# Reordering the prologue of an FFT convolution followed by two feed-forward layers

## The chip, the cores and the metric

The kernel runs on one core of one Trainium2 chip. The metric is the device time of one execution in microseconds (us). The kernel before took 1052.2 us (median of 3 runs, 1052.01 to 1052.93).

Five engines work side by side, each through its own list of instructions in order, and wait for each other by semaphores: TensorE (PE, matrix products), VectorE (DVE), ScalarE (ACT), GpSimd (POOL) and SyncE (SP, which here only issues DMAs).

## The reference, cut to what matters

```python
def _attn_ref(x, filt_r, filt_i):            # x: 2 x 3008 x 256
    X = np.fft.rfft(x, axis=1)
    Y = X * (filt_r + 1j * filt_i)[None, :, :]
    return np.fft.irfft(Y, n=x.shape[1], axis=1)

x = _attn_ref(x, ...).reshape(6016, 256)
h = x @ moe_w_in                             # 256 -> 2048
g = np.where(h > 0, h, np.exp(np.minimum(h, 0)) - 1)
x = g @ moe_w_out                            # 2048 -> 256
h = x @ moe2_w_in
g = h * np.clip(h + 3, 0, 6) / 6
return g @ moe2_w_out
```

A Fourier transform along each of two sequences, a complex product with a filter, the transform back, and two feed-forward layers on the 6016 rows that come out.

## The kernel before

The transform of length 3008 is split as 47 times 64, so that it becomes small matrix products with a transpose between them. A sequence is treated in two halves of 128 columns (h is 0 or 1). For the first sequence, whose work the change moves, each half goes through these steps; the letters are those of the string `PROLOGUE`, and the digits behind a letter are h and the group g:

- **A** (`s1t`): products with the 47-point table, five columns at a time, copied from PSUM into the tile zt. Seven groups; those of half 0 stand ahead of the string.
- **T** (`tr`): four transposes into one PSUM bank, and a copy out of it. Six groups a half.
- **S** (`s2_mm`, then `mult`): the 64-point product on PE (line 204), then the complex product with the filter: three VectorE multiplications (lines 216, 216, 217) and an addition on GpSimd (line 219).
- **I** (`i2_mm`, `i2_evac`): the inverse 64-point product (line 224), a ScalarE copy (line 234) and a DMA to a buffer in DRAM (line 235).
- **V** (`v_load`): four DMAs that read the half back from DRAM (line 239), transposed on the way. All six groups I of the half must have landed.
- **O** or **o** (`i1_mm`, `i1_evac`): the inverse 47-point products (line 247), seven groups a half, copied out on ScalarE (O) or VectorE (o) into the blocks from which the first layer reads.

Between them stand: **F**, the sign of a filter group on GpSimd (line 149), without which its complex product can't start; **c** and **k**, steps of the generators `lead` and `conv`, which turn chunks of the first layer's weights (int64 words of a double) into two rounded floats; **w**, the DMA of a raw chunk; **M**, the split of a table into two rounded floats; **x**, **b**, **B**, the load, the split and the first product of the second sequence; **X**, the split of a block into two rounded floats (line 85 has VectorE's half); **G** and **H**, the first and second half of the first layer's product of a block with chunk 0.

A chunk's conversion is five VectorE operations (lines 299, 300, 304, 306, 308) and one on ScalarE (297), then one ScalarE rounding (314) and two VectorE operations (316, 318). Chunk 0 must be ready before G.

Behind the string come the 96 units of the main loop, each of six first-layer products (lines 88 to 90), an ELU on ScalarE and VectorE (lines 497, 498, 500), a split (lines 84, 85) and, three units later, twelve second-layer products. From there on the two kernels hold the same instructions in the same order.

The order on each engine is the order in which the program issues it; nothing reschedules it. PSUM has seven banks in turn, so an instruction may also wait until a bank is read out. SP issues DMAs in the program's order, and each of its DMAs waits until the eighth before it has landed.

Of the kernel before, what the change touches and what calls it, by code (L numbers as in the profile page):

```python
# [47 lines left out]
def fft_conv_moe_moe2(ctx, tc, xp, fq, sg, cs1, cs1t, cs2, ci2, ci1, ident, w1i, w1o, w2i, w2o, out):  # L48
    nc = tc.nc
# [11 lines left out]
    def name(s):  # L61
        uid[0] += 1
        return f"{s}_{uid[0]}"
# [7 lines left out]
    def bank():  # L71
        return ps.tile([P, 512], F32, tag="ps", name=name("ps"))
# [81 lines left out]
    def s1t(b, h, jg, eng):  # L154
        if jg == 0:
            zt[h] = p12.tile([P, NK2, 2, 2, NJ], F32, tag="zt", name=name("zt"))
        acc = bank()
        j0, n = jg * TG, min(TG, NJ - jg * TG)
        for j in range(j0, j0 + n):
            nc.tensor.matmul(  # L160
                acc[:, (j - j0) * KP : (j - j0 + 1) * KP], xin[b, h, j // 8][:KP, j % 8, :],
                mats["s1t"][:KP], start=True, stop=True,
            )
        evac(
            eng,
            zt[h].rearrange("p k c h j -> p (c h) k j")[:, :, :, j0 : j0 + n],
            acc[:, : n * KP].rearrange("p (j c k) -> p c k j", j=n, c=4),
        )

    def tr(b, h, g, eng):  # L170
        acc = bank()
        for k in range(4):
            nc.tensor.transpose(
                acc[:, k * P : (k + 1) * P],
                zt[h][:, 4 * g + k].rearrange("p c h j -> p (c h j)"), mats["id"],
            )
        zs[b, h, g] = t2([P, 512])
        evac(eng, zs[b, h, g], acc)
# [665 lines left out]
    def fetch1(f):  # L844
# [9 lines left out]


    PROLOGUE = """
        T00 T01 T02 S00 T03 F01 S01 T04 F01 S02 T05 F01 S03 I00 F01 S04 I01 F01 A10 A11 F01
        S05 I02 A12 A13 A14 I03 F01 A15 A16 I04 T10 c01 T11 c01 w00 I05 F01 x00 x01 V00 T12
        S10 T13 S11 T14 F01 S12 T15 S13 I10 F01 S14 I11 S15 I12 O00 I13 b00 c01 O01 I14 c01
        b01 o02 O03 I15 M00 c01 b02 V10 c01 X00 O04 w01 b03 c01 X01 k02 O05 O06 X02 k02 B00  # L860
        B01 B02 B03 G00 G01 k03 O10 o11 G02 X10 o12 X11 O13 X12 o14 k02 H00 H01 k02 O15 k01
        H02 O16
    """
    LOADS = [(0, None, q, None) for q in range(4)]
    for x in "F00 F01 F02 F03 X0 X1 X2 X3 F04 F05 F10 W0 M F11 F12 F13 F14 F15".split():
# [150 lines left out]
    with tc.manual_schedule():  # L1016
        for key, src in (("s1t", cs1t), ("id", ident), ("sg", sg), ("s2", cs2), ("i2", ci2), ("i1", ci1)):
            load_mat(key, src)
        three = const.tile([P, 1], F32, name="three")
        nc.vector.memset(three, 3.0)  # L1020
        engs = (nc.scalar, nc.vector)

        acc = bank()
        for n in WARM:
            zeros = (nc.const_aps.tensor(0.0, [P, k], F32) for k in (P, n))
            nc.tensor.matmul(acc[:, :n], *zeros, start=True, stop=True)
        for h, g, q, r in LOADS:
            if q is not None:
                x_load(0, h, q)
            elif g is not None:  # L1030
                f_load(0, h, g)
            elif r is not None:
                w_raw(0, r)
            else:
                load_mat("s1", cs1, nc.sync)
        for jg in range(JG):
            s1t(0, 0, jg, engs[jg % 2])
        lead = w_chain(0, WLEAD, lambda f: None)
        f_sign(0, 0, 0)
        f_sign(0, 0, 1)  # L1040
        nsign = 2
        for step in PROLOGUE.split():
            what, h, g = step[:-2], int(step[-2]), int(step[-1])
            if what == "T":
                tr(0, h, g, nc.scalar if g > 1 else engs[g])
            elif what == "S":
                s2_mm(0, h, g)
                mult(0, h, g)
            elif what == "A":
                s1t(0, h, g, engs[g % 2])  # L1050
            elif what == "I":
                i2_mm(0, h, g)
                i2_evac(0, h, g)
            elif what == "V":
                for q in range(4):
                    v_load(0, h, q)
            elif what == "O":
                i1_mm(0, h, g)
                i1_evac(0, h, g, nc.scalar)
            elif what == "o":  # L1060
                i1_mm(0, h, g)
                i1_evac(0, h, g, nc.vector)
            elif what == "k":
                steps(conv, g)
            elif what == "c":
                steps(lead, g)
            elif what == "X":
                x_split(0, g, h)
            elif what == "F":
                for _ in range(g):  # L1070
                    f_sign(0, *divmod(nsign, 6))
                    nsign += 1
            elif what == "x":
                x_load(1, h, g)
            elif what == "w":
                w_raw(0, WLEAD + g)
            elif what == "b":
                s1_split(h, g)
            elif what == "B":
                s1_mm(1, h, g, parts.pop(("x", h, g)))  # L1080
                s1_evac(1, h, g)
            elif what == "G":
                g1_half(units[g], 0)
            elif what == "H":
                g1(units[g])
                if g:
                    g_split(units[g - 1])
            elif what == "M":
                split_mat("s1")

        for n, u in enumerate(units):
            place[0] = n
            for fn in pre[n]:
                fn()
            if n >= NI:
                g1(u)
                g_split(units[n - 1])
            if n >= SKEW:
                g2(units[n - SKEW])
            for fn in post[n]:  # L1100
                fn()
        def rest(n):
            def run():
                if n == NU:
                    g_split(units[-1])
                g2(units[n - SKEW])
                for fn in post[n]:
                    fn()
            return run

        old = None
        n = place[0] = NU
        for l, p in ROUNDS:
            for q in range(GROUPS):
                old = group(l, p, q, old, [rest(NU + i) for i in range(3)], pre[n : n + 4])
                n += 4
        prod(old.l, old.p, old.q, 3, old.c, False)
        old.high((1, 1))
        old.gate((1, 0))
        old.add((0, 1), old.u2, old.c)  # L1120
        old.low((1, 1))
        old.high((1, 0))
        old.relu((0, 1))
        old.low((1, 0))
        old.gate((0, 1))
        old.high((0, 1))
        old.low((0, 1))
        for key in ((0, 0), (1, 1), (1, 0), (0, 1)):
            old.second(key)
            if key == (1, 0):  # L1130
                out_evac(old.l, old.p, 0)
        out_evac(old.l, old.p, 1, True)
# [82 lines left out]
```

## Time and profile before

| | |
|---|---|
| median of 3 runs | 1052.2 us |
| the profiled execution | 1053.41 us, of which span 1051.6 us |
| PE busy | 1039.5 us (99%) |
| VectorE busy | 880.3 us (84%) |
| ScalarE busy | 807.4 us (77%) |
| GpSimd busy | 195.4 us (19%) |
| TensorE clock granted | 1.00 of full speed throughout |

The string's work lies in the first 72 us of the span. A timeline row names the start, the duration and the instruction, and in brackets how long the engine had been idle before it and what ended that. Matrix products are pipelined: a row's duration holds about 0.16 us of pipeline, so that the distance from start to start is the price of a product.

### The profile page before, as it was taken

The page shows a single profiled execution, that of the slowest core. Times are in us where ns is not written, and L with a number is a line of the kernel's source. Part 1 is how long each engine was busy: PE and PEld are TensorE (multiplying, and loading weights), DVE is VectorE, ACT ScalarE, POOL GpSimd, SP SyncE. Part 2 cuts the span into 40 slices and gives each one's busy share as a digit, 9 for nine tenths or more (in the row PEclk, how much of TensorE's full clock was granted, in tenths as well). Part 3 has the DMA queues.
Part 4 walks back from the last instruction along what each step waited for, and adds up shares of the span by engine and source line. Part 5 has one row for each costly group of instructions (what it writes and reads, how often), then busy time and mean ns, then how long its engine had stood idle before and what let it go on. Part 6 is the DMA issues. An engine that isn't in the chain of part 4 may idle for free.

```text
span 1051.6 us, 14389 instructions
## 1 busy us (share of the span) xinstructions
PE 1039.5 (99%) x5022; PEld 913.4 (87%) x5022; DVE 880.3 (84%) x1416; ACT 807.4 (77%) x1453; POOL 195.4 (19%) x211
## 2 busy tenths in 40 slices
PE   9999999999999999999999999999999999999998
PEld 6688888888889989988888888888888888888998
DVE  4899999789986888789989888888888888787776
ACT  3488888997777888888987877777777777777766
POOL 3700001425545933200011100010010010000000
PEclk9999999999999999999999999999999999999999
DMA  9993100474655543510564631100100100100100
GB/s 285 307 273 128 46 1 1 154 222 150 203 168 176 202 140 121 178 41 1 187 234 122 216 123 41 41 21 21 41 21 21 41 18 17 41 1 1 41 2 35
DMA packets 58056, 107.31 MB, mean 102 GB/s; under 512 B 5024, under 2 KB 33696, under 8 KB 57984
## 3 DMA queue, kind: packets, MB, share of 16 engines
q1 hardware_dynamic: 52112, 88.16, 25.5%
q0 software_dynamic: 4896, 17.83, 5.4%
q8 instruction: 39, 0.64, 0.3%
q10 hardware_dynamic: 976, 0.41, 0.2%
q14 instruction: 33, 0.27, 0.1%
HBM read 69.42 MB, written 36.96 MB: 101 GB/s over the span
## 4 chain that ended last, share of the span: by engine, by line
PE 85%; DVE 6%; DMA 4%; ACT 3%; issue 1%; POOL 0%; ACTq 0%; SPq 0%; DVEq 0%
PE ps L88 25%; PE ps L90 25%; PE ps L89 25%; PE lone L88 3%; PE lone L89 3%; PE lone L90 3%; PE ps L247 2%; DMA t<-in_fq 2%; DMA scr<-t 1%; DMA t<-scr 1%; DVE t L679 1%; PE ps L224 1%; DVE t L85 1%; DVE t L692 1%; DVE t L647 1%
## 5 line engine op out<-in xcount | busy, mean ns | idle before, releaser
L88 PE MATMUL ps<-t,w 128*128 128x512 f32 (+1 forms) x1072 | 403.4, 376 | 2.9 <-DVE t L217 1.9
L90 PE MATMUL ps<-t,w 128*128 128x512 f32 (+1 forms) x1072 | 402.2, 375 | 0.8 <-DVE t L692 0.6
L89 PE MATMUL ps<-t,w 128*128 128x512 f32 (+1 forms) x1072 | 401.8, 375 | 0.3 <-DVE w L318 0.2
L88 PEld LDWEIGHTS ps<-t,w 128*128 128x128 f32 x1072 | 202.9, 189 | 28.7 <-DVE t L500 1.7
L90 PEld LDWEIGHTS ps<-t,w 128*128 128x128 f32 x1072 | 202.8, 189 | 26.8 <-DVE t L692 2.8
L89 PEld LDWEIGHTS ps<-t,w 128*128 128x128 f32 x1072 | 202.9, 189 | 24.6 <-DVE w L318 1.7
L692 DVE TENSOR_TENSOR t<-t,t 128x512 fp32r<-128x512 f32 (+1 forms) x256 | 175.4, 698 | 26.9 <-ACT t L687 25.2
L687 ACT ACTIVATE t<-t 128x512 fp32r<-128x512 f32 (+1 forms) x256 | 154.3, 616 | 6.1 <-DVE t L677 5.7
L641 ACT ACTIVATE t<-ps 128x512 f32<-128x512 f32 (+1 forms) x175 | 102.6, 586 | 62.4 <-PE ps L90 60.6
L661 ACT ACTIVATE t<-t,three 128x512 f32<-128x512 f32 (+1 forms) x143 | 96.6, 707 | 38.4 <-DVE t L647 37.7
L677 DVE SCALAR_TENSOR_TENSOR t<-t,t 128x512 f32<-128x512 f32 (+1 forms) x143 | 96.8, 703 | 33.3 <-ACT t L661 32.8
L497 ACT ACTIVATE t<-ps 128x512 f32<-128x512 f32 (+1 forms) x128 | 74.3, 580 | 46.8 <-PE ps L90 38.4
L647 DVE TENSOR_TENSOR t<-ps,t 128x512 f32<-128x512 f32 (+1 forms) x128 | 86.5, 676 | 11.6 <-ACT t L641 11.0
L498 ACT ACTIVATE t<-t 128x512 f32<-128x512 f32 (+1 forms) x128 | 79.2, 619 | 4.1
L85 DVE TENSOR_TENSOR t<-t,t 128x512 fp32r<-128x512 f32 (+2 forms) x96 | 70.2, 735 | 4.0 <-ACT t L84 3.9
L500 DVE SCALAR_TENSOR_TENSOR ps<-t,ps 128x512 f32<-128x512 f32 (+1 forms) x76 | 50.3, 662 | 27.8 <-ACT t L498 27.4
L84 ACT ACTIVATE t<-t 128x512 fp32r<-128x512 f32 (+2 forms) x108 | 65.0, 616 | 3.1 <-DVE t L81 2.0
L561 POOL TENSOR_TENSOR t<-t,t 128x512 f32<-128x512 f32 (+1 forms) x12 | 16.2, 1352 | 253.5 <-DVE t L647 224.4
L88 PE MATMUL ps<-t,t 128*128 128x512 f32 (+1 forms) x160 | 60.4, 377 | 0.0
L90 PE MATMUL ps<-t,t 128*128 128x512 f32 (+1 forms) x160 | 60.1, 376 | 0.0
L89 PE MATMUL ps<-t,t 128*128 128x512 f32 (+1 forms) x160 | 60.1, 376 | 0.0
L88 PE MATMUL lone<-t,w 128*128 128x512 f32 (+1 forms) x144 | 54.1, 376 | 0.0
(118 smaller groups left out, 1612.6 us busy)
## 6 DMA issues: line engine op xcount, KB each, us to landing
t<-in_fq SPq DMA_DIRECT2D x24, 512.0 KB, 6.4
scrw<-t SPq DMA_DIRECT2D x16, 512.0 KB, 3.0
w<-scrw POOLq DMA_DIRECT2D x16, 512.0 KB, 4.6
scr<-t SPq DMA_DIRECT2D x24, 256.0 KB, 3.7
t<-scr SPq DMA_DIRECT2D x16, 384.0 KB, 5.2
t<-in_xp SPq DMA_DIRECT2D x15, 384.0 KB, 5.9
scrx<-t SPq DMA_DIRECT2D x10, 512.0 KB, 2.7
t<-scr POOLq DMA_DIRECT2D x10, 512.0 KB, 6.2
```

Source lines behind the costliest of these rows:

```text
L85: eng.tensor_tensor(out=lo, in0=src, in1=_f32(hi), op=ALU.subtract)
L88: nc.tensor.matmul(acc, wh, xh, start=start, stop=False, skip_group_check=more)
L89: nc.tensor.matmul(acc, wl, xh, start=False, stop=False, skip_group_check=more)
L90: nc.tensor.matmul(acc, wh, xl, start=False, stop=stop, skip_group_check=more)
L497: nc.scalar.activation(r, acc, AF.Relu, scale=-1.0)
L498: nc.scalar.activation(t[:, :n], t[:, :n], AF.Exp, scale=-1.0)
L641: nc.scalar.activation(like(t, self.n), got(bank_, self.n), AF.Copy)
L647: nc.vector.tensor_tensor(out=like(self.h[key], n), in0=got(bank_, n), in1=like(u, n), op=ALU.add)
L661: nc.scalar.activation(like(r, n), h, AF.Relu, bias=three)
L677: stt(out=r, in0=r, scalar=6.0, in1=h, op0=ALU.min, op1=ALU.mult)
L687: nc.scalar.activation(gh[:, : self.n], g[:, : self.n], AF.Copy)
L692: nc.vector.tensor_tensor(out=gl[:, :n], in0=g[:, :n], in1=_f32(gh[:, :n]), op=ALU.subtract)
```

## The change

The string `PROLOGUE` is written anew with the same steps but for their order and for which engine copies some results. Two lines of the loop that reads it change the engine: of the T groups only the first goes to VectorE, and all A groups go to ScalarE.

```diff
     PROLOGUE = """
-        T00 T01 T02 S00 T03 F01 S01 T04 F01 S02 T05 F01 S03 I00 F01 S04 I01 F01 A10 A11 F01
-        S05 I02 A12 A13 A14 I03 F01 A15 A16 I04 T10 c01 T11 c01 w00 I05 F01 x00 x01 V00 T12
-        S10 T13 S11 T14 F01 S12 T15 S13 I10 F01 S14 I11 S15 I12 O00 I13 b00 c01 O01 I14 c01
-        b01 o02 O03 I15 M00 c01 b02 V10 c01 X00 O04 w01 b03 c01 X01 k02 O05 O06 X02 k02 B00
-        B01 B02 B03 G00 G01 k03 O10 o11 G02 X10 o12 X11 O13 X12 o14 k02 H00 H01 k02 O15 k01
-        H02 O16
+        T00 F01 T01 T02 T03 T04 S00 T05 S01 F01 S02 F01 F01 S03 A10 S04 A11 F01 A12 A13 A14 w00
+        A15 S05 A16 I00 T10 F01 M00 F01 c01 F01 T11 T12 c01 T13 F01 x00 S10 S11 I01 I02 c01 c01
+        S12 I03 I04 b00 I05 S13 k01 I10 c01 I11 k01 T14 F01 V00 T15 I12 S14 B00 S15 c01 I13 b01
+        k01 O00 O01 X00 k01 c01 I14 O02 I15 X01 x01 O03 k01 X02 w01 o04 V10 k01 G00 k01 b02 b03
+        G01 O05 o06 B01 G02 k01 k01 B02 B03 O10 O11 k01 k01 k01 X10 o12 O13 X11 H00 X12 O14 o15
+        H01 o16 H02
     """
@@
             if what == "T":
-                tr(0, h, g, nc.scalar if g > 1 else engs[g])
+                tr(0, h, g, nc.scalar if h or g else nc.vector)
@@
             elif what == "A":
-                s1t(0, h, g, engs[g % 2])
+                s1t(0, h, g, nc.scalar)
```

VectorE before, from the fourth complex product of the second half to the first weight operation behind the sixth:

```order
L216 TENSOR_TENSOR t_123_495<-ps_492,t_20_165 64x512 x2
L217 TENSOR_TENSOR t_122_494<-ps_492,t_20_165 128x512
L216 TENSOR_TENSOR t_129_510<-ps_507,t_21_167 64x512 x2
L217 TENSOR_TENSOR t_128_509<-ps_507,t_21_167 128x512
L216 TENSOR_TENSOR t_135_524<-ps_521,t_22_169 64x512 x2
L217 TENSOR_TENSOR t_134_523<-ps_521,t_22_169 128x512
L85 TENSOR_TENSOR t_144_549<-t_95_424,t_143_548 96x512
L304 SCALAR_TENSOR_TENSOR t_87_402<-raw_156,t_88_403 128x512
```

VectorE after the change, from behind the second complex product of the second half to the start of the fifth:

```order
L304 SCALAR_TENSOR_TENSOR t_80_389<-raw_156,t_81_390 128x512
L306 TENSOR_SCALAR t_81_390<-t_80_389 128x512
L216 TENSOR_TENSOR t_104_453<-ps_450,t_19_163 64x512 x2
L217 TENSOR_TENSOR t_103_452<-ps_450,t_19_163 128x512
L85 TENSOR_TENSOR t_111_470<-t_89_418,t_110_469 96x512
L216 TENSOR_TENSOR t_116_481<-ps_478,t_20_165 64x512 x2
L217 TENSOR_TENSOR t_115_480<-ps_478,t_20_165 128x512
L308 SCALAR_TENSOR_TENSOR t_82_391<-raw_156,t_81_390 128x512
L299 TENSOR_SCALAR t_119_490<-t_119_490 128x512
L300 TENSOR_SCALAR t_120_491<-t_119_490 128x512
L216 TENSOR_TENSOR t_138_538<-ps_535,t_21_167 64x512 x2
```

The weight operations of chunk 0, and the first two of chunk 1, now stand between the complex products instead of behind the last. On PE, five of the first half's six inverse products (groups 1 to 5) have moved in between the second half's 64-point products; before, all six stood ahead of the first of them.

VectorE before, at the first three ELUs (line 500; line 85 splits their results, line 81 is a copy of an O group):

```order
L299 TENSOR_SCALAR t_198_757<-t_198_757 128x512
L300 TENSOR_SCALAR t_199_758<-t_198_757 128x512
L500 SCALAR_TENSOR_TENSOR t_201_766<-t_201_766,ps_692 128x512
L500 SCALAR_TENSOR_TENSOR t_202_773<-t_202_773,ps_696 128x512
L85 TENSOR_TENSOR t_204_778<-t_201_766,t_203_777 128x512
L304 SCALAR_TENSOR_TENSOR t_198_757<-raw_628,t_199_758 128x512
L306 TENSOR_SCALAR t_199_758<-t_198_757 128x512
L308 SCALAR_TENSOR_TENSOR t_200_759<-raw_628,t_199_758 128x512
L500 SCALAR_TENSOR_TENSOR t_206_795<-t_206_795,ps_720 128x512
```

VectorE after the change, at the same three:

```order
L500 SCALAR_TENSOR_TENSOR t_200_759<-t_200_759,ps_657 128x512
L85 TENSOR_TENSOR t_169_631<-t_160_607,t_168_630 128x512
L81 COPY t_172_644<-ps_773 128x210
L81 COPY t_185_681<-ps_773 128x260
L500 SCALAR_TENSOR_TENSOR t_203_784<-t_203_784,ps_670 128x512
L85 TENSOR_TENSOR t_205_789<-t_200_759,t_204_788 128x512
L81 COPY t_185_681<-ps_792 128x188
L500 SCALAR_TENSOR_TENSOR t_207_799<-t_207_799,ps_693 128x512
```

All five operations of chunk 2 have moved ahead of the first ELU; copies of O groups stand in their place. From the third ELU on both orders are the same.

SP before, from the last two writes of the second half to the loads behind its read back (scr_0_1 is the second half's buffer in DRAM):

```order
L235 DMA scr_0_1_83<-t_148_564 128x4x128
L235 DMA scr_0_1_83<-t_156_592 128x4x128
L239 DMA t_159_604<-scr_0_1_83 96x1024
L239 DMA t_160_606<-scr_0_1_83 96x1024
L239 DMA t_161_608<-scr_0_1_83 96x1024
L239 DMA t_162_610<-scr_0_1_83 96x1024
L269 DMA raw_628<-in_w1i 128x2x256
```

SP after the change, at the same writes:

```order
L235 DMA scr_0_1_83<-t_158_597 128x4x128
L235 DMA scr_0_1_83<-t_162_611 128x4x128
L140 DMA t_165_618<-in_xp 96x1024
L269 DMA raw_634<-in_w1i 128x2x256
L273 DMA raw_634<-in_w1o 128x512
L239 DMA t_173_646<-scr_0_1_83 96x1024
L239 DMA t_174_648<-scr_0_1_83 96x1024
```

A load of the second sequence (384 KB) and a raw weight chunk (512 KB) now stand between the last write and the read back.

## Rows read from the trace of the kernel before

**Rows 1.** Stretches: PE, PEld, DVE, ACT, POOL busy us (instructions), clock, DMA share, GB/s.

```profile
28.50:47.05 18.55, 17.57 (x82) 10.45 (x83) 14.73 (x24) 8.20 (x15) 12.34 (x12) 1.00 0.94 304
...
80.56:120.00 39.44, 39.44 (x183) 34.51 (x184) 38.33 (x66) 32.62 (x56) 0.00 (x0) 1.00 0.27 90
```

**Rows 2.** PE timeline: start, duration, instruction, idle before it and releaser.

```profile
13.86 1.53 PE L173 MATMUL ps<-id,zt 128*128 128x128 f32 x12 [0.42 <-ACT zt L79]
...
47.05 1.32 PE L247 MATMUL ps<-i,t 96*128 96x94 f32 x10 [0.53 <-DMA t<-scr]
...
53.29 1.05 PE L224 MATMUL ps<-t,i 128*128 128x512 f32 x2
...
61.68 2.44 PE L247 MATMUL ps<-i,t 96*128 96x94 f32 x20 [0.80 <-DMA t<-scr]
...
71.42 0.46 PE L88 MATMUL ps<-t,w 128*128 128x512 f32 x1
...
80.56 0.48 PE L88 MATMUL ps<-t,w 128*128 128x512 f32 x1 [0.75 <-DVE t L500]
```

**Rows 3.** Chain of waits between 26 and 75 us: start, duration, piece.

```profile
31.93 1.54 PE ps L160 x14
...
36.53 0.86 PE ps L204 x2
...
38.69 0.44 PE ps L173 x4
...
41.28 0.89 PE ps L224 x2
...
42.74 4.17 DMA t<-scr
...
49.27 1.09 PE ps L247 x10
...
57.40 4.15 DMA t<-scr
```

**Rows 4.** VectorE timeline, columns as in the PE timeline.

```profile
26.41 1.39 DVE L216 TENSOR_TENSOR t<-ps,t 64x512 f32<-64x512 f32 x2 [1.19 <-POOL t L149]
...
37.48 1.39 DVE L216 TENSOR_TENSOR t<-ps,t 64x512 f32<-64x512 f32 x2 [0.51 <-PE ps L204]
...
49.76 0.69 DVE L217 TENSOR_TENSOR t<-ps,t 128x512 f32<-128x512 f32 x1
...
74.74 0.68 DVE L500 SCALAR_TENSOR_TENSOR t<-t,ps 128x512 f32<-128x512 f32 x1
...
79.83 0.68 DVE L500 SCALAR_TENSOR_TENSOR t<-t,ps 128x512 f32<-128x512 f32 x1
```

**Rows 5.** VectorE groups, 54 to 92 us: line, shapes, count, busy, mean ns.

```profile
L304 DVE SCALAR_TENSOR_TENSOR t<-raw,t 128x512 uint32<-128x512 uint32 x4 | 3.1, 774 | 0.0
...
L300 DVE TENSOR_SCALAR t<-t 128x512 uint32<-128x512 uint32 x5 | 2.1, 427 | 0.2
...
L306 DVE TENSOR_SCALAR t<-t 128x512 uint32<-128x512 uint32 x4 | 1.7, 422 | 0.1
```

**Rows 6.** The same three groups, 340 to 370 us, where GpSimd works.

```profile
L304 DVE SCALAR_TENSOR_TENSOR t<-raw,t 128x512 uint32<-128x512 uint32 x3 | 3.5, 1163 | 0.0
L300 DVE TENSOR_SCALAR t<-t 128x512 uint32<-128x512 uint32 x3 | 3.3, 1087 | 0.2
...
L306 DVE TENSOR_SCALAR t<-t 128x512 uint32<-128x512 uint32 x2 | 1.0, 498 | 0.0
```

**Rows 7.** GpSimd timeline: the sum of one complex product.

```profile
48.28 1.27 POOL L219 TENSOR_TENSOR t<-t,t 128x512 f32<-128x512 f32 x1
```

**Rows 8.** SP timeline: issue of the last write of each half.

```profile
37.11 0.38 SPq L235 DMA_DIRECT2D scr<-t  x1
...
55.00 0.36 SPq L235 DMA_DIRECT2D scr<-t  x1
```

**Rows 9.** Line 300 over the whole span: duration in ns, min/median/max.

```profile
L300 DVE TENSOR_SCALAR t<-t x32: 426/427/1387, 36.5 to 556.0; 128x512 uint32<-128x512 uint32 x32
```

## The prediction, as recorded before the change was run

> **What bounds the kernel now.** I read the engine table first, then the main loop's start, then the first 81 us one engine at a time. PE is busy for 99% of the span, and from 80.56 us on it has no idle time worth a name: 39.44 of 39.44 us, 183 products, 0.2155 us each [rows 1]. Both kernels hold the same instructions in the same order there, so the end moves by as much as PE reaches that point sooner or later. What counts is the prologue, and in it PE's waits, since its products are the same before and after. The reader is to see three of them: 0.53 us at 47.05, 0.80 us at 61.68, 0.75 us at 80.56 [rows 2]. The first two end with a read back from DRAM (V), the third with an ELU on VectorE. So the prologue is held by two round trips, each from the last inverse product of a half over its copy, its write and its read, and at its end by VectorE's backlog.
>
> VectorE sets when the second round trip can start. Its six complex products of the second half run back to back from 37.48 to 49.76 + 0.69 = 50.45 us, 2.16 us each [rows 4]; the last inverse product follows at 53.29 [rows 2]. From its start to the issue of its write pass 55.00 - 53.29 = 1.71 us [rows 2, 8], to the read 57.40 - 55.00 = 2.40, to the first O product 61.68 - 57.40 = 4.28: 8.39 in all [rows 2, 3, 8].
>
> **The prices.** T 0.44 us, S 0.86, I 0.89, O 1.09 for five columns, A 1.54 / 7 = 0.22 a column [rows 3]; B, G and H three products, 0.65 [rows 1]. No matrix product is added or removed. Some copies out of PSUM go from VectorE to ScalarE, a few the other way; I cost that at nothing, since ScalarE hides it (8.20 of 18.55 us busy where most of them fall [rows 1]).
>
> **First point, the first O product (47.05 before).** In the new order stand ahead of it 12 T, 12 S, all 32 columns of A, 10 I (six of half 0, four of half 1) and one B: 5.28 + 10.32 + 7.04 + 8.90 + 0.65 = 32.2 us from 13.86, so PE arrives at 46.1 if it never waits [rows 2]. For the first half's filters nothing is sooner: the fifth complex product waits until 26.41 for its sign [rows 4], in either order. The data: the last inverse product of half 0 comes later than before, behind 10 T, 9 S, A and 5 I: 4.40 + 7.74 + 7.04 + 4.45 = 23.6, at 37.5; its write is issued 1.71 later, at 39.2. It needed 42.74 - 37.11 = 5.63 us to land before, with a raw chunk just ahead of it and two loads behind, and the half-1 write needed 2.40 [rows 3, 8]. I take 3.0, near the lower, since the raw chunk is now some 10 us ahead. The read stands behind two half-1 writes in SP's queue, the later of which is issued at about 41.9; so 42.2 to 42.4, and 4.31 on (47.05 - 42.74): 46.7. With 5.63 it would be 49.1. At 46.7 PE is 0.35 us earlier and has done one I and one B more, 1.54 us: a lead of 1.9.
>
> **Second point, the first O product of half 1 (61.68 before).** The first complex product of half 1 can start when its S is through: 13.86 + 4.40 + 5.16 + 7.04 + 0.89 + 0.86 = 32.2, with 0.3 to the next engine 32.5, five us sooner than before. But between the six there now stand six weight and split operations: lines 304, 306, 308, 299, 300 and one of line 85, 3.5 us by the undisturbed means (0.77 twice, 0.42 and 0.43, 0.42 for line 299 as its twin, 0.69) [rows 5]. 32.5 + 6 x 2.16 + 3.5 = 49.0. Two more, 299 and 300 of chunk 0, stand just ahead of the first product.
>
> They pay for their place: GpSimd is at work through most of this stretch (signs, sums: 12.34 of 18.55 us [rows 1]). Where it works, line 300 takes 1087 ns for 427, line 304 1163 for 774, line 306 498 for 422 [rows 5, 6]. For eight operations: twice 0.66, once 0.39, five times 0.14 (nearer to line 306, the mildest row) make 2.4 us. With none it is 0; with line 300's largest excess for all, 1387 - 427 = 0.96, it is 7.7 [rows 9]. I take 2.4. The last complex product then ends at 51.4, later than before, its sum 1.35 us on (1.27 and a start of 0.08) [rows 7], and the last inverse product starts at 52.8, against 53.29.
>
> The round trip of 8.39 gives 61.2. In SP's queue a load of 384 KB and a raw chunk of 512 KB now stand between the write and the read: 0 if they move while the write is being acknowledged, 5.63 - 2.40 = 3.2 if they cost what the raw chunk and loads cost the first write; I take 0.3, since the write is issued ahead of them. 61.5. PE arrives about then: 52.8 + 0.89 + three O and a short one (3.71) + three G and three B (3.90) = 61.3. It has done one G more than before (0.65). Lead: 0.18 + 0.65 = 0.8.
>
> **Third point, the seventh unit (80.56 before).** From 61.68 to the main loop at 71.42 are 9.74 us [rows 2], of which the G is now done: 61.5 + 9.1 = 70.6. The third ELU started at 74.74, 3.3 us after that point, because VectorE still had chunk 2 to convert [rows 2, 4]. Three of these operations, 0.77 + 0.42 + 0.77 = 1.96, are now done before the first ELU, so that 1.4 us are left at least, 3.3 at most if the copies in their place take as long; I take 2.0. Third ELU 72.6; to the end of the fifth 80.51 - 74.74 = 5.8 as before: 78.4. PE without a wait needs 80.56 - 0.91 - 71.42 = 8.2 us (the wait is 0.75 and 0.16 of pipeline) and arrives at 78.8. It does not wait. Lead: 80.56 - 78.8 = 1.8.
>
> **The sum.** 1.9 at the first point, 0.8 at the second, and 1.0 given back at the third because VectorE's backlog is gone: 1.8 us. The profiled execution took 1053.41 us, 1.81 of it outside the span of 1051.6; the span would be 1049.8 and the execution 1051.6. It lay 1.2 above the median, so for the median 1052.2 - 1.8 = 1050.4.
>
> [...] Here conversions lengthen beside GpSimd by 0.08 to 0.66 us on average [rows 5, 6]. [...]
>
> **The rivals.**
>
> 1. The conversions are not stretched. For: undisturbed they are short, and complex products, which read one side from PSUM, show no stretch [rows 4]. Then the last inverse product starts as soon as PE reaches it, at 46.7 + 3 x 1.09 + 0.89 = 50.9; the round trip ends at 59.3 to 59.6, a lead of 2.7, and with 0.9 at the third point 3.6: 1048.6. With half the stretch it is 1049.2.
> 2. Slower: all eight conversions pay what line 300 pays, 0.66 us, 5.3 in all. The place is VectorE between the second half's complex products, and the last inverse product starts 2.9 us later than in the forecast: 1053.3. It decides from 4.2 us of stretch (0.5 each): below, the kernel is not slower. At 0.96 each it is 1055.7. For: GpSimd is hardly idle there. Against: line 306's row.
> 3. The order does nothing: DMA, not order, sets both reads (5.63 us for the first write, 3.2 for what now stands ahead of the second read). The second read then ends at 61.2 + 3.2 = 64.4, the lead there is -2.7 + 0.65 = -2.1, and the third point gives 1.0 to 1.9 back: 1052.4 to 1053.3. For: the DMA engines are 0.94 busy where both stand [rows 1]. [...]
>
> **How the numbers follow.** Forecast 0.45, with its own range 1049.7 to 1051.4; rival 1 0.29; rival 2 0.14; rival 3 0.12. The range 1048.7 to 1053.2 takes in the first rival up to its clean end and the second about to its price. What a measurement of this kernel can tell from no change is about 0.2%, 2.1 us, so faster means below 1050.1: nearly all of rival 1 and a quarter of the forecast, 0.39. Slower means above 1054.3: half of rival 2 and a part of rival 3, 0.10. The same: 0.51.
>
> **What would show it.** The first O product at 46.7 with one B done; the second half's complex products from 32.5 to about 51.4, with lines 299 to 308 between them at 0.5 to 1.1 us; the last inverse product at 52.8; half 1's first O product at 61.5; the main loop at 70.6; no wait for line 500 at the seventh unit. The prediction is wrong if a wait of more than a microsecond stands anywhere in front of these, if the conversions stay at their undisturbed times (then it is too slow), or if the read of half 1 is issued more than 4 us after its last write.

## The result, and the profile after

The changed kernel took 1057.36 us (median of 10 runs, 1054.48 to 1064.29) against 1052.38 us (10 runs, 1051.98 to 1052.99). The ratio is 1.0063 with a 95% interval of 1.004 to 1.0087: slower by 5 us. The profiled execution took 1057.69 us, 1055.9 of it the span. From 84.82 us on it does what the kernel before does from 80.56 us on [rows 2], so the loss of 4.3 us lies ahead of that point.

PE after the change, timeline from 36 to 92 us, columns as in [rows 2]:

```profile
43.03 1.09 PE L173 MATMUL ps<-id,zt 128*128 128x128 f32 x8 [1.31 <-DVE t L217]
44.75 1.12 PE L224 MATMUL ps<-t,i 128*128 128x512 f32 x2 [0.63 <-POOL t L219]
...
48.94 2.37 PE L247 MATMUL ps<-i,t 96*128 96x94 f32 x20
52.47 2.01 PE L224 MATMUL ps<-t,i 128*128 128x512 f32 x2 [1.16 <-POOL t L219]
54.28 2.06 PE L247 MATMUL ps<-i,t 96*128 96x94 f32 x10
56.18 1.05 PE L224 MATMUL ps<-t,i 128*128 128x512 f32 x2
...
67.08 4.67 PE L247 MATMUL ps<-i,t 96*128 96x94 f32 x40 [0.99 <-DMA t<-scr]
...
84.82 0.48 PE L88 MATMUL ps<-t,w 128*128 128x512 f32 x1 [0.53 <-DVE t L500]
```

Against [rows 2]: the first O product stands at 48.94 (47.05 before), the last inverse product at 56.18 (53.29), the first O product of half 1 at 67.08 (61.68). New are waits of 0.6 us and more for the complex products (releasers L217 and L219; none of that kind was over 0.26 before), and one inverse product that takes 2.01 us where its like takes 1.05. For that the clock is read, two stretches of the same profile (columns as in [rows 1]):

```profile
52.00:54.00 2.00, 1.53 (x2) 0.78 (x3) 1.97 (x4) 0.48 (x1) 1.08 (x2) 0.64 0.48 134
54.00:56.00 2.00, 2.00 (x10) 1.72 (x9) 2.00 (x3) 0.60 (x1) 0.89 (x1) 0.51 0.00 0
```

Behind the wait of 1.16 us TensorE's granted clock fell to about half of full speed (0.64 from 52 to 54 us, 0.51 from 54 to 56), for about 3.5 us. In the kernel before it was 1.00 throughout.

VectorE, from the table's split to the last complex product:

```profile
30.59 0.34 DVE L122 CAST s_h<-s 128x96 fp32r<-128x96 f32 x1
30.96 1.24 DVE L123 TENSOR_TENSOR s_l<-s,s_h 128x96 fp32r<-128x96 f32 x1
32.12 1.26 DVE L299 TENSOR_SCALAR t<-t 128x512 f32<-128x512 f32 x1
33.42 1.15 DVE L300 TENSOR_SCALAR t<-t 128x512 uint32<-128x512 uint32 x1
34.59 1.39 DVE L216 TENSOR_TENSOR t<-ps,t 64x512 f32<-64x512 f32 x2
...
38.73 0.68 DVE L304 SCALAR_TENSOR_TENSOR t<-raw,t 128x512 uint32<-128x512 uint32 x1
39.45 1.37 DVE L306 TENSOR_SCALAR t<-t 128x512 uint32<-128x512 uint32 x1
...
42.89 0.68 DVE L85 TENSOR_TENSOR t<-t,t 96x512 fp32r<-96x512 f32 x1
...
45.60 0.68 DVE L308 SCALAR_TENSOR_TENSOR t<-raw,t 128x512 f32<-128x512 uint32 x1
46.19 1.50 DVE L299 TENSOR_SCALAR t<-t 128x512 f32<-128x512 f32 x1
47.80 1.07 DVE L300 TENSOR_SCALAR t<-t 128x512 uint32<-128x512 uint32 x1
...
52.47 0.69 DVE L217 TENSOR_TENSOR t<-ps,t 128x512 f32<-128x512 f32 x1
```

and GpSimd in the same place:

```profile
38.96 1.58 POOL L219 TENSOR_TENSOR t<-t,t 128x512 f32<-128x512 f32 x1 [0.85 <-DVE t L217]
...
45.82 1.59 POOL L219 TENSOR_TENSOR t<-t,t 128x512 f32<-128x512 f32 x1 [1.13 <-DVE t L217]
47.36 1.23 POOL L149 TENSOR_TENSOR t<-t,sg 128x512 f32<-128x512 f32 x1
...
53.33 1.55 POOL L219 TENSOR_TENSOR t<-t,t 128x512 f32<-128x512 f32 x1 [0.92 <-DVE t L217]
```

Read the two together: line 306 starts at 39.45 inside GpSimd's sum, which runs from 38.96 to 40.54, and ends at 40.82. Line 299 at 46.19 lies in the sum that ends at 47.41 and ends at 47.69; line 300 behind it in the sign that ends at 48.59. Line 304 at 38.73 is there before the sum, takes its undisturbed 0.68, and the sum takes 1.58 instead of 1.27 [rows 7]. The first complex product of half 1 starts at 34.59 and the last ends at 53.16 (37.48 and 50.45 before [rows 4]).

SP's queue around the two reads back (line 239):

```profile
39.87 0.36 SPq L235 DMA_DIRECT2D scr<-t  x1
40.32 0.46 SPq L269 DMA_DIRECT2D raw<-in_w1i  x1
40.83 0.48 SPq L273 DMA_DIRECT2D raw<-in_w1o  x1
41.77 0.98 SPq L235 DMA_DIRECT2D scr<-t  x2
42.94 3.71 SPq L239 DMA_DIRECT2D t<-scr  x4
...
57.89 0.36 SPq L235 DMA_DIRECT2D scr<-t  x1
58.35 0.44 SPq L140 DMA_DIRECT2D t<-in_xp  x1
58.89 0.38 SPq L269 DMA_DIRECT2D raw<-in_w1i  x1
...
60.62 1.73 SPq L239 DMA_DIRECT2D t<-scr  x4
```

From the second read's issue to its first product pass 67.08 - 60.62 = 6.46 us (4.28 before). And behind half 0's last write a raw chunk (lines 269, 273) goes ahead of the first read: chunk 3, which the first step k of chunk 1 loads. The two writes at 41.77, of half 1, stand ahead of that read too.

Three causes offer themselves, all in one chain: conversions stretched between the complex products; loads ahead of the reads; the clock, which fell to 0.51 behind PE's wait of 1.16 us. A fourth is that the inverse products put off make the first read late.

### The profile page after: what moved, and what is told of

It reads as the page before. It is cut to its first block, busy times and chain, and to the rows that moved or that the text cites. A ratio compares the mean times of both kernels' runs of the same rounds, so it can differ in the third digit from the quotient of the medians.

```text
span 1055.9 us, 14394 instructions
## 1 busy us (share of the span) xinstructions
PE 1041.2 (99%) x5022; PEld 913.9 (87%) x5022; DVE 882.6 (84%) x1412; ACT 809.0 (77%) x1457; POOL 197.4 (19%) x211
## 4 chain that ended last, share of the span: by engine, by line
PE 84%; DVE 6%; DMA 5%; ACT 3%; issue 1%; POOL 0%; SPq 0%; ACTq 0%; DVEq 0%; POOLq 0%
PE ps L90 25%; PE ps L88 25%; PE ps L89 24%; PE lone L88 3%; PE lone L89 3%; PE lone L90 3%; PE ps L247 2%; DMA raw<-in_w1o 2%; DMA t<-in_xp 1%; DVE t L679 1%; DMA t<-scr 1%; DVE t L85 1%; DVE t L692 1%; DVE t L647 1%; DVE t L216 1%
```

## The experiments

Twelve kernels. The diffs show only the steps of the string that move; `z` is a step of three of the experiments (3, 5 and 12), products of zeros whose result nobody reads (`z12`: one of 256 columns, `z13`: of 384, `z14`: of 512).

**1. The read ahead of the loads.**

```diff
-c01 I13 b01 ... I15 X01 x01 O03 k01 X02 w01 o04 V10 k01
+c01 I13 x01 b01 ... I15 V10 X01 O03 k01 X02 w01 o04 k01
```

> The changed kernel with only SP's queue altered: the load of the second sequence stands between the fourth and fifth write of half 1 instead of behind the last, and the read back of half 1 stands right behind its last write, ahead of the raw chunk. If the loads that stood between write and read cost the read its time (6.46 us from its issue to the first O product against 4.28 before), the last write is still issued near 57.9, the read near 60.3, the first O product of half 1 stands near 64.6 instead of 67.08 and the time is about 2.5 us under the changed kernel's: 1054.9. If the queue's order costs nothing and the delay is all from the late last inverse product, it stays at 1057.4.

1065.02 us, ratio 1.0116 (1.0102 to 1.013): a miss. ScalarE's timeline, then PE's:

```profile
71.45 0.66 ACT L297 ACTIVATE t<-raw 128x512 f32<-128x512 f32 x1 [6.28 <-DMA raw<-in_w1o]
```

```profile
72.64 4.40 PE L247 MATMUL ps<-i,t 96*128 96x94 f32 x20 [3.95 <-ACT t L190]
```

Chunk 2's first operation stood on ScalarE waiting for the raw chunk that I had put behind the read, and two copies of banks (line 190) waited behind it, and PE for a bank. The clock was 0.53 from 72 to 86 us. Since the change converts chunk 2 sooner, its load can't go behind the read.

**2. The conversions behind the complex products.**

```diff
-T10 F01 M00 F01 c01 F01 T11 T12 c01 T13 ... I02 c01 c01 S12 I03 I04 b00 I05 S13 k01 I10 c01 I11 k01 ... S14 B00 S15 c01 I13 b01 k01 O00 O01 X00 k01
+T10 F01 F01 c01 F01 T11 T12 T13 ... I02 S12 I03 I04 I05 S13 k01 I10 I11 ... S14 S15 M00 c01 c01 I13 b00 c01 c01 k01 O00 O01 B00 X00 c01 b01 k01 k01
```

> The changed kernel with the split of the table, the five conversion steps, the block split and the first product of the second sequence put behind the last complex product of half 1, so that VectorE does the six back to back. If conversions between them, stretched beside GpSimd, are what makes the last inverse product late (56.18), the first complex product starts near 32.1 and the last ends near 46 instead of 53.16, the last inverse product moves up to about 52.4, the first O product of half 1 to about 63.3 and the time is 3.8 us lower: 1053.6; PE no longer waits over a microsecond and the granted clock stays at 1.00. If the conversions only fill time that is lost anyway (the read of half 0, which gives the first O product at 48.94, or DMA sets it), it stays within a microsecond of 1057.4.

1060.63 us (1056.19 to 1067.57), ratio 1.0082 (1.005 to 1.0114). The last complex product ended at 48.17, 5 us sooner. PE's timeline:

```profile
48.52 4.17 PE L247 MATMUL ps<-i,t 96*128 96x94 f32 x20 [2.93 <-DMA t<-scr]
...
56.73 1.05 PE L224 MATMUL ps<-t,i 128*128 128x512 f32 x2
```

The rival was right in this: the read of half 0 (issued 42.70, 5.82 us) is as late as VectorE was. The time saved became a PE wait of 2.93 us; the clock was 0.62 from 48 to 52 and 0.52 to 56, and the last inverse product stood where it had.

**3. PE kept busy in its waits.**

```diff
-I02 c01 c01 S12 ... k01 T14 F01 ... T15 I12 ... c01 I14 O02
+I02 c01 c01 z12 S12 ... k01 z14 T14 F01 ... T15 z12 I12 ... c01 z14 I14 O02
```

> The changed kernel with four products of zeros more on PE, into a bank that nobody reads, each placed just ahead of one of the four waits of half 1 (0.60, 1.31, 0.63 and 1.16 us) and shorter than it or about as long. If PE's waits are what let the granted clock fall to half at 52 to 56 us, it stays at 1.00, the inverse product at 52.47 takes 1.05 instead of 2.01 and the O group behind it 1.3 instead of 2.06, the last inverse product starts about 1.3 us sooner, the time falls by 1.3 to 2 us to about 1055.6 and the ten times of the kernel, spread over 10 us, come within 1. If the clock falls for another reason, time and spread stay as they are, or the products cost up to 0.5 us where they overrun a wait.

1056.61 us (five of six runs from 1056.23 to 1057.34, one of 1061.99), ratio 1.0048 (1.0032 to 1.0065). PE, and the clock from 52 to 54 us:

```profile
52.79 1.02 PE L224 MATMUL ps<-t,i 128*128 128x512 f32 x2
...
54.93 1.13 PE L224 MATMUL ps<-t,i 128*128 128x512 f32 x2
...
65.20 4.67 PE L247 MATMUL ps<-i,t 96*128 96x94 f32 x40 [0.84 <-DMA t<-scr]
```

```profile
52.00:54.00 2.00, 2.00 (x9) 1.03 (x9) 1.97 (x4) 1.29 (x4) 1.13 (x2) 1.00 0.74 221
```

More work on PE, and the clock stayed at 1.00, the last inverse product came 1.25 us sooner and half 1's first O product 1.9. The span is 1.5 us shorter. The median is 0.75 lower, less than expected and not clear of noise: the intervals overlap. The two runs of the change at a clock of 1.000 took 1054.48 and 1055.95, the five here at 0.999 and 1.000 from 1056.23 to 1057.34, so the products of zeros may cost time of their own. What is shown is that with PE's waits filled the clock was 1.00 from 52 to 56 us, where the change had 0.64 and 0.51, not what the fall costs in the median; the one long run (mean clock 0.994) had lost some of its clock all the same.

**4. Edits 1 and 2 together.** The string has both diffs.

> Both edits together: conversions behind the last complex product, and the read of half 1 right behind its last write. If the two costs are separate they add up: first O product of half 1 near 60.8, time 1057.4 - 3.8 - 2.5 = 1051.1, a microsecond under the kernel before. If only one of them is real it equals the better of the two alone (1053.6 or 1054.9). If the conversions, now in a bunch ahead of the first layer's products, become the bound there (chunk 0 is needed at the first G), the gain is less and a wait for VectorE stands at the first G.

1066.6 us, ratio 1.0134 (1.0121 to 1.0147). It has the waits of both (3.31 us for the read of half 0, 3.40 for line 190), and tells nothing more.

**5. Filled, and the loads in the DMA pause.**

```diff
-c01 I13 b01 ... I15 X01 x01 O03 k01 X02 w01 o04 V10 k01
+c01 I13 x01 w01 b01 ... I15 V10 X01 O03 k01 X02 o04 k01
```

(and the four `z` of the third experiment)

> The changed kernel with the four products of zeros in PE's waits (the clock held at 1.00, as in the third experiment) and with the load of the second sequence and the raw chunk both behind the inverse product of group 3 of half 1, so that they move while the DMA engines are idle (52 to 58 us), and the read of half 1 right behind its last write. If the 896 KB between write and read cost the read its 2.2 us, then against the third experiment (1056.6, first O product of half 1 at 65.20) the first O product stands near 63.0, the first product that needs the second sequence's load does not wait, and the time is 1054.4. If the read is late only because its write is, nothing changes: 1056.6.

1054.52 us (11 runs, 1054.05 to 1055.47), ratio 1.0021 (1.0012 to 1.003). SP's queue, then PE:

```profile
56.77 0.37 SPq L235 DMA_DIRECT2D scr<-t  x1
59.25 2.07 SPq L239 DMA_DIRECT2D t<-scr  x4
```

```profile
63.61 4.60 PE L247 MATMUL ps<-i,t 96*128 96x94 f32 x40
```

The read took at most 63.61 - 59.25 = 4.36 us (PE did not wait for it), against 65.20 - 59.44 = 5.76 in the third experiment and 6.46 in the change, and the time fell by 2.1 us as expected. The loads' price is shown; the mean clock was 0.999 or 1.000 in all eleven runs, and 2.1 us over before are left.

**6. GpSimd without work in half 1.** The signs and sums of half 1 are left out.

```diff
-        nc.gpsimd.tensor_tensor(out=ws[b, h, g], in0=u, in1=v, op=ALU.add)
+        if h and not b:
+            ws[b, h, g] = u
+        else:
+            nc.gpsimd.tensor_tensor(out=ws[b, h, g], in0=u, in1=v, op=ALU.add)
```

> The changed kernel without GpSimd's work in the second half of the first sequence: its signs and its sums are left out (the inverse products read one part of the complex product). If GpSimd is what stretches VectorE's weight and split operations, lines 299, 300 and 306 take 0.43 us each instead of 1.07 to 1.50, s_l 0.26 instead of 1.24 and the last complex product ends near 48 instead of 53.16. If DMA traffic or the place in the program stretches them, they stay above a microsecond.

VectorE (lines 303, 304 and 310 here are 299, 300 and 306), then PE:

```profile
32.04 0.41 DVE L303 TENSOR_SCALAR t<-t 128x512 f32<-128x512 f32 x1
32.49 0.43 DVE L304 TENSOR_SCALAR t<-t 128x512 uint32<-128x512 uint32 x1
...
37.82 0.43 DVE L310 TENSOR_SCALAR t<-t 128x512 uint32<-128x512 uint32 x1
...
48.16 0.69 DVE L218 TENSOR_TENSOR t<-ps,t 128x512 f32<-128x512 f32 x1
```

```profile
48.23 2.87 PE L251 MATMUL ps<-i,t 96*128 96x94 f32 x20 [2.45 <-DMA t<-scr]
```

GpSimd is the stretch: without it the five take 0.40 to 0.43 us (1.07 to 1.50 in the change) at DMA shares as high (1.00 to 1.09 from 32 to 48 us, 0.96 to 1.11 in the change), and the last complex product ends at 48.85. Only s_l still takes 1.38, beside half 0's last sum. The time, 1057.46 us (1055.28 to 1063.91), is no better: the read of half 0 gives the first O product at 48.23, and the clock falls (0.76 from 48 to 52).

**7. The kernel before, its inverse products put off.**

```diff
-S03 I00 F01 S04 I01 ... S05 I02 A12 A13 A14 I03 F01 A15 A16 I04 T10 ... I05 F01 x00 x01 V00 T12 S10 T13 S11 T14 F01 S12 T15 S13 I10 F01 S14 I11 S15
+S03 F01 S04 ... S05 A12 A13 A14 F01 A15 A16 I00 T10 ... F01 x00 x01 T12 S10 T13 S11 I01 I02 T14 F01 S12 I03 I04 I05 T15 S13 I10 F01 S14 I11 V00 S15
```

> The kernel before with one part of the change: five of the six inverse products of half 0 stand between the second half's 64-point products, the conversions stay where they were. The six complex products of half 1 then run back to back from about 32 to 45 us. The last write of half 0 is issued near 40.5 and the read near 43.5, so that the first O product comes at about 47.8 behind a PE wait of 3 us (47.05 before). If that wait leaves the clock alone, the time is 0.7 us over before: 1053.1. If a wait of over a microsecond lets the granted clock fall, as at 52 us after the change, 2 to 10 us more: 1055 to 1063. If putting them off is the good part of the change, the sooner complex products bring it under 1051.

1065.28 us (1058.55 to 1071.42), ratio 1.012 (1.0079 to 1.0161). PE:

```profile
50.92 1.80 PE L247 MATMUL ps<-i,t 96*128 96x94 f32 x10 [4.20 <-DMA t<-scr]
```

This order cost more than expected: PE waited 4.20 us for the read, and the clock fell (0.62 from 52 to 56). But it isn't the price of putting them off alone. The edit also puts the read behind two writes of half 1, and the later of these, issued at 45.66, let the read go at 46.26 only, not near 43.5. And the complex products ran from 35.16 to 49.18, not from 32 to 45: PE had waited 2.00 us at 31.74 for a copy on VectorE (line 81).

**8. The kernel before, its conversions sooner.**

```diff
-T12 S10 T13 S11 T14 F01 S12 T15 S13 I10 F01 S14 I11 S15 I12 O00 I13 b00 c01 O01 I14 c01 ... I15 M00 c01 b02 V10 c01 ... b03 c01 X01 k02
+M00 T12 S10 T13 S11 c01 c01 T14 F01 S12 b00 T15 S13 k01 I10 F01 c01 S14 I11 k01 S15 I12 c01 O00 I13 O01 I14 c01 ... I15 b02 V10 ... b03 X01
```

> The kernel before with the other part of the change: the table's split, chunk 0's conversion, a block split and the first operations of chunk 1 stand between the complex products of half 1, the inverse products where they were. If conversions between the complex products are what makes the changed kernel late, the last complex product ends 6 to 8 us after 50.45, the last inverse product stands near 60 instead of 53.29, PE waits over a microsecond in front of inverse products, and the time is 1056 to 1060, more where the clock falls. If they only use gaps in VectorE's work, it stays within a microsecond of 1052.4 or gains the 0.75 us of the wait at the seventh unit.

1056.16 us (1055.71 to 1059.56), ratio 1.0042 (1.0026 to 1.0057). VectorE:

```profile
42.87 1.37 DVE L306 TENSOR_SCALAR t<-t 128x512 uint32<-128x512 uint32 x1
...
52.21 1.30 DVE L300 TENSOR_SCALAR t<-t 128x512 uint32<-128x512 uint32 x1
...
54.93 0.69 DVE L217 TENSOR_TENSOR t<-ps,t 128x512 f32<-128x512 f32 x1
```

The last complex product ends at 55.62, 5.2 us late (a little under the 6 to 8 expected). The six weight and split operations among the complex products took 5.13 us; 1.82 of it is stretch, the rest their undisturbed time. The last inverse product stands at 60.22; that it meets the "near 60" is luck, since in this profiled run PE waited 1.51 us for GpSimd at 48.14 and the clock was 0.58, 0.50 and 0.64 in the 4 us stretches from 48 to 60. The three runs that were only timed had a mean clock of 0.999 and still took 1055.71 to 1056.27: this part alone costs 3.6 us at a clock near full (1056.04, their median, against 1052.41).

**9. Edit 2, and no raw chunk ahead of the read of half 0.**

```diff
-I05 S13 k01 I10 I11 T14 F01 V00 T15 ... b00 c01 c01 k01
+I05 V00 S13 I10 I11 T14 F01 T15 ... b00 c01 c01 k02
```

> The second experiment (conversions behind the last complex product) with one more edit: the read of half 0 stands right behind that half's last write, and the first step of chunk 1, which issues the 512 KB of chunk 3, is put behind the read instead of ahead of it. In the second experiment PE stood 2.93 us in front of the first O product (48.52). If the raw chunk and the two half-1 writes ahead of the read make it late, the read is issued near 42.3 and the first O product stands near 46.6, PE waits about a microsecond there, the last inverse product moves up by some 2 us from 56.73, and where the clock holds the time is 2 to 4 us under the second experiment's best (1056.2): 1052 to 1054. If the read is bound by the landing of the last write or by DMA traffic as such, the first O product stays near 48.5 and the time near 1057.

1064.19 us (1057.7 to 1067.08): a miss, and inconclusive. In the profiled run the clock was down to 0.50 from 12 to 20 us, ahead of all that was edited, so that the read was issued at 46.49 and the first O product stood at 50.53, not near 42.3 and 46.6. The read itself took 4.04 us and PE waited 0.37 for it; but now PE waited 0.77 and 1.80 us for the table's and the block's split, and the clock fell again (0.50 from 56 to 72 us).

**10. All three in one order.**

```diff
-F01 M00 F01 c01 F01 T11 T12 c01 T13 ... I02 c01 c01 S12 I03 I04 b00 I05 S13 k01 I10 c01 I11 k01 T14 F01 V00 T15 I12 S14 B00 S15 c01 I13 b01 k01 O00 O01 ...
+F01 F01 c01 F01 T11 T12 T13 ... I02 S12 I03 T14 I04 I05 V00 S13 T15 F01 S14 I10 I11 S15 I12 I13 x01 w01 I14 c01 M00 c01 b00 O00 c01 O01 c01 b01 I15 V10 ...
```

(Behind these, X, b, B, c, k, O and G stand in a new order too.)

> A version made from what the runs showed, without added products: the changed kernel's order up to the third complex product of half 1, then no conversion or split among the complex products, the read of half 0 right behind its last write, inverse products 0 to 4 of half 1 ahead of the first O product so that PE has work while the read is on its way, the second sequence's load and the raw chunk of chunk 2 behind the write of group 3, and the read of half 1 right behind its last write. The complex products run from about 32 to 45.5, the first O product stands near 46.6 without a wait of a microsecond, the last inverse product near 49, the read of half 1 is over before PE has done its other work (near 59), so that the second wait is gone, the clock stays at 1.00 in all runs and the time is 1050 to 1051.5, 1 to 2 us under the kernel before. If the reads still set the pace or the conversions in a bunch come late for the first G (PE waits for VectorE near 57), it is 1053 or more.

1054.7 us (1053.76 to 1062.48), ratio 1.0027 (1.0012 to 1.0041). First O product at 46.53 (4.46 us after its read's issue) and last inverse product at 48.81, as expected; but the last write, behind x01 and w01, landed late, PE waited 0.82 and 0.52 us for splits of the second sequence's load, and the clock fell to 0.61 from 60 to 64. The time expected, 1050 to 1051.5, is missed. SP, its issue and that of the read:

```profile
51.85 1.14 SPq L235 DMA_DIRECT2D scr<-t  x1
58.72 1.26 SPq L239 DMA_DIRECT2D t<-scr  x3
```

**11. Its two loads moved.**

```diff
-x00 S10 ... I13 x01 w01 I14 ... I15 V10
+x00 x01 S10 ... I13 I14 ... I15 w01 V10
```

> The version before with its two loads moved once more. There the last write of half 1, issued at 52.6 behind 896 KB of loads, took until 58.72 to land (2.3 to 2.7 where no load stood ahead), so that the first O product of half 1 came at 63.26 behind a PE wait in which the clock fell, and two products of the second sequence waited 0.82 and 0.52 us for its load. Now the second sequence's load stands beside the first such load (near 31 us, so that it moves while the DMA engines are half idle at 40 to 44) and the raw chunk between the last write and the read of half 1. The last write should land near 53.5, the read be issued near 54 and the first O product of half 1 stand where PE reaches it, at 59 to 60, with no wait; the clock stays at 1.00 and the time is 1050 to 1051. If the second load delays the read of half 0 instead (first O product at 48 rather than 46.53, PE waiting over a microsecond), or the raw chunk the read of half 1, it is 1052 to 1054.

PE:

```profile
47.03 2.44 PE L247 MATMUL ps<-i,t 96*128 96x94 f32 x20 [0.75 <-DMA t<-scr]
...
60.66 4.67 PE L247 MATMUL ps<-i,t 96*128 96x94 f32 x40 [0.90 <-DMA t<-scr]
...
78.41 0.48 PE L88 MATMUL ps<-t,w 128*128 128x512 f32 x1 [0.53 <-DVE t L500]
```

The profiled run's span is 1049.5 us, 2.1 under before, its seventh unit 2.15 us sooner than in [rows 2]. Neither wait for a read is gone: the read of half 1 was issued at 56.90, behind the raw chunk, not near 54. And of the twelve runs (1051.13 to 1061.74, median 1052.73) four had a mean clock of 0.990 to 0.996 and took 1055 to 1062. Ratio 1.0018 (0.9996 to 1.0041): no gain is shown.

**12. Its two waits filled.**

```diff
-b00 O00 ... G02 k01 O10
+b00 z13 O00 ... G02 k01 z14 O10
```

> The version before with two products of zeros more, into a bank that nobody reads, one just ahead of each of its two remaining waits for a read (0.75 us at 47.03, filled with 0.65 us; 0.90 us at 60.66, filled with 0.86). Its twelve times ran from 1051.13 to 1061.74, the long ones at a granted clock of 0.990 to 0.996. If even these short waits now and then let the clock fall, the clock now is 0.999 or 1.000 in every run, the times lie within 2 us and their median is near the best of the version before: 1051.2, some 1.2 us under the kernel before. If the long runs have another cause, runs of 1055 and over remain and the median stays near 1052.7.

1052.32 us (1051.67 to 1063.19), ratio 1.0002 (0.9983 to 1.0021). Ten of twelve runs lie within 1.4 us, one took 1063.19 at a clock of 0.990. In the profiled run half 0's last write took 5.1 us to land (39.43 to 44.53, against 39.13 to 42.77 in experiment 11), and PE waited 1.37 us after all. No version is shown to beat the kernel before.

## Why the prediction was wrong

It said 1050.4, and slower than 1054.3 with a chance of 0.10; it was 1057.4. The direction was wrong. Three terms were too small (the stretch, the loads ahead of the read of half 1, the read of half 0), and two were left out (the table's split, the clock).

- **First point (46.7 forecast, 48.94).** For the landing of half 0's last write, "I take 3.0, near the lower, since the raw chunk is now some 10 us ahead", the trace has 2.5 us from its issue at 39.87; the read went at 42.94, behind the two half-1 writes, some 0.5 us after the 42.2 to 42.4 of the forecast. The step behind it failed: 4.31 us for the read. One raw chunk was 10 us ahead, but another stood right ahead of the read; I had counted step k as VectorE work and left out the DMA that it issues. With that chunk there the read took 5.55, 5.82 and 6.44 us (experiments 6, 2 and 3), without it 4.46 and 4.26 (10 and 11); since the two half-1 writes were gone from ahead of it as well, the chunk's own share is not separated. PE came as late by itself, behind 2.5 us of waits for VectorE and GpSimd.
- **Second point (61.5 forecast, 67.08): where it was lost.** "I take 2.4" for the stretch of eight operations was 4.0: they took 8.39 us against 4.35 undisturbed. A further 1.1 came from the table's split (1.58 for 0.46), which I had not placed there at all. Most of this was lost ahead of the first complex product, where I had taken the start from PE's products alone: the split and lines 299 and 300 took 3.99 us there for 1.31, and the product started at 34.59 rather than 32.5. From there to the end of the sixth passed 18.57 us, with 18.9 forecast. GpSimd's last sum took 1.55 for 1.27. So the last inverse product could start at 54.93 (experiment 3) rather than 52.8: 2.13 us. The clock made that 56.18: 1.25 us. The write was issued 1.71 us later, as forecast. "I take 0.3" for the two loads held for its landing (2.73 for 2.40); on the read itself, where I had put nothing, they cost 2.18 (6.46 for 4.28), of which experiment 5 gave back 1.4 against the third and 2.1 against the change. No run shows a pause behind the write in which both loads could move, on which the 0.3 stands: before, the DMA share was 0.00 only from 57.0 us to the read's issue at 57.40, and in the change it was 1.06 from 60.0 to 60.5 us and 1.26 from there to 61, around the read's issue at 60.62. 2.13 + 1.25 + 2.18 is all but 0.02 of the 5.58 us. I gave no row for the 0.3 us "to the next engine" nor for the 0.08 ahead of the sum; before, half 1's first complex product started 0.26 us after the 0.86 of its product (36.36 and 37.48), and the sums that waited for VectorE 0.09 to 0.14 us behind it.
- **Third point.** Right in size: 17.74 us from half 1's first O product to the seventh unit, against 18.88 before and 17.3 forecast. But VectorE's wait did not go; 0.53 of 0.75 us stayed.
- **The clock** had no term. Every wait was priced at its length. Multiplying each of the ten times by its run's mean clock gives 1053.2 to 1056.0, mean 1054.5: an estimate by which the clock took 2.9 us of the median and 2.1 are left over before. As many are left in experiment 5, where the loads are moved as well; so this estimate and the experiments do not add up to shares of the 5 us.
- **The rivals.** Rivals 2 and 3 each named a real cause and gave 1053.3 and 1052.4 to 1053.3. Neither held whole: the eight operations' 4.0 us of stretch lie just under the 4.2 from which rival 2 was to decide, and of rival 3 the second read was late, but the first write landed in 2.5 us, not 5.63. I had made them alternatives; they sit in one chain and add up. With the table's split the stretch is 5.1 us. Where the two engines met, line 306, begun at 39.45 inside GpSimd's sum, took 1.37 us for 0.42 and ended 0.28 us behind the sum's end at 40.54; that sum, begun at 38.96 inside line 304, took 1.58 for 1.27. I had priced the stretch by the means of a later part of the run [rows 6], and those do not tell which engine came first.

Shown by runs of their own are the stretch (6), the price of conversions in that place (8), the price of the loads (5) and the clock with PE's waits and without (3: 1.00 for 0.64 and 0.51). Taking the stretch away did not make the changed kernel faster by itself (2 and 6): PE then waited 2.93 and 2.45 us for the read of half 0, and the clock fell (0.62 and 0.76 from 48 to 52 us). What putting the inverse products off costs is not separated: experiment 7 moved the read with them. The copies that went to ScalarE, which I costed at nothing, have no run of their own either; in the profile after, ScalarE ends no wait of PE of 0.5 us or more before 64.17. Why single runs still lose the clock when the known waits are filled is open.

## What to carry to other kernels

Work that is "off the path" wasn't free here, in a chain of VectorE's and GpSimd's short steps: five VectorE operations took 1.07 to 1.50 us beside GpSimd's work and 0.40 to 0.43 without it (the change and experiment 6). So try long VectorE operations where GpSimd is idle, or ahead of its start (there line 304 took 0.68, and it was the sum that took 1.58 us for 1.27). That alone did not make this kernel faster. Of a step that moves, list the DMAs too, and ask which write or read they come to stand in front of. And a wait of PE cost more than its length where the clock fell behind it (1.16 us in the change, and 1.25 more up to the last inverse product); compare single times with their clock before reading a difference of 0.5%.

## What the runs showed of the hardware that was not expected

The granted clock fell behind waits of PE for VectorE, GpSimd or ScalarE: 1.16 us (the change), 1.04 (experiment 1), 1.51 (8), 1.80 (9) and 0.52 (10), each the last of several. It also fell behind waits for DMA of 2.45 to 4.20 (experiments 6, 2, 4 and 7). At 0.50 to 0.57 of full speed products took about twice their time (2.01 us for 1.05 in the change), for 3.5 us in the change and some 20 in experiment 9 (0.50 from 56 to 72 us, 0.59 to 76). The length of a single wait did not tell: 1.31 (the change, at 43.03), 1.37 (experiment 12, at 48.59) and 2.00 us (experiment 7, at 31.74) left the clock at 1.00. Products of zeros in the waits of the change held it at 1.00 in the profile (3).

A 256 KB write took 2.4 to 3.0 us from its issue to the read that waits for it (55.00 to 57.40 before, 56.77 to 59.25 in experiment 5, 39.11 to 42.07 in experiment 10), 3.6 to 5.6 for half 0 before and in experiments 11 and 12, and 6.9 behind 896 KB of loads (51.85 to 58.72, experiment 10). A read that PE waited for took 3.8 to 4.7 us to its first product, and 5.5 to 6.5 where 512 to 896 KB of loads had been issued less than 2 us ahead of it; in experiment 11 the raw chunk ahead of the read of half 1 had been issued 2.6 us before it, and the read took 3.76.
